# Retention followed by a multiplicative FFN: attention by units of a chunk of two batches, with products grouped by tiling mode

## The chip, the cores and the metric

The kernel runs on one core of a Trainium2 chip. The metric is the device time of the program in microseconds (us). A core has five engines that run side by side, each through its own instructions in order: TensorE (PE in the profile; its weight loads are PEld), VectorE (DVE), ScalarE (ACT), GpSimd (POOL) and SyncE (SP), which here only issues transfers. TensorE's results go to PSUM, eight banks of 2 KB on each of 128 partitions; everything else lies in SBUF.

## The reference, cut to what matters

```python
def _attn_ref(q, k, v):                      # (8, 8, 576, 64) each: batch, head, position, dim
    scores = (1 / sqrt(64)) * (q @ k.T)
    gamma = 1.0 - 2.0 ** (-5.0 - arange(8))  # one a head
    rel = i - j
    Dmat = where(rel >= 0, gamma ** rel, 0.0)
    return (scores * Dmat) @ v

def reference(...):
    x = attn_out.transpose(0, 2, 1, 3).reshape(4608, 512)
    a = x @ w1                               # 512 x 1024
    b = x @ w2                               # 512 x 1024
    h = (a * b) @ w3                         # 1024 x 1024
    return h @ w_out                         # 1024 x 512
```

The weights are float64; the kernel reads their 32-bit words and makes float32 of them on the chip. All products are in float32; each shows as two MATMUL records in the trace (two passes).

## The kernel before, in words

**Retention by chunks.** Each batch of 576 positions is cut into five chunks (`NC`), the first of 64 positions and four of 128. Because gamma^(i-j) = gamma^i * gamma^-j, the kernel scales q by gamma^i / 8 and v by gamma^-j and needs three things for a chunk: scores within the chunk, masked to j <= i, times v; q times the state, which is the sum of k v^T over the earlier chunks; and the state's own growth. The result is made transposed, (head, dim) on partitions, four pairs of heads (`NP`) of 128 rows each, as the FFN takes it.

The unit of attention is one chunk of one batch, 40 units `g`, and four functions make it:

- `front(g)` (line 105): GpSimd scales v (L110), TensorE transposes k and q in pairs of heads into `tp` tiles (L118), ScalarE copies k's out (L122), VectorE copies q's out and scales them on the way (L124, with `gq`, which eight broadcast loads, L86, fill at the start).
- `score(g)` (line 127): per pair of heads two products (L135), the first on the upper 64 rows of the array and the second on the lower 64, into two PSUM tiles `sc0` and `sc1`; VectorE multiplies by the mask into `pm` (L138).
- `state(g)` (line 142): eight products (L154) of 128 rows on the left or right 64 columns of the array grow the state in its own PSUM bank, which ScalarE copies to `sb` (L158) for the next chunk.
- `pv(g)` (line 161): for each head in turn a product of the state with q on a 64x64 quarter (L171, only two of the four quarters are ever used), and right behind it the product of v with the masked scores on a 128x64 half (L173), both added up in one PSUM tile `xps`, which ScalarE copies to `xT` (L176).

**Weights.** 40 blocks of 128 rows by 512 columns: 8 + 8 of w1 and w2, 8 of w_out, 16 of w3. `load_block` (L199) loads one on SP's queue into one of three `raw` tiles, `convert_block` (L209) makes float32 of it in seven VectorE instructions (L219 to L231) and starts the next load. w3 and w_out are multiplied out once: `w3_tr` (L241) transposes a row block of w3 on TensorE (L247), `w3_mm` (L253) makes the product (L256).

**FFN.** A pair of batches has 1152 tokens, three blocks (`NB`) of 384. `up(i, n, f)` (L266) makes 128 columns of x w1 and x w2 with four products each (L275); ScalarE copies the first (L279) and VectorE multiplies it with the second into `ab` (L280). `down(i, n, t)` (L282) makes 128 tokens of output with eight products (L286), ScalarE copies them out (L289), SP stores them (L291). A block has eight `up`s and three `down`s.

**The order is written out by hand** (`manual_schedule`): each engine does its instructions in the order in which the program emits them. The loop from line 315 goes over the units: it loads unit g+3, converts up to five blocks ahead, does `front(g+2)`, then a third of the FFN work due in this unit, `score(g+1)` and `state(g+1)`, a third, `pv(g)`, and the last third. After the last chunk of the first batch of a pair one FFN block comes due, after that of the second the other two; the w3 steps stand in the first pair's list, behind the first eight `up`s. PSUM is split into pools: two banks for transposes, two for scores, one for the state, three for everything else (lines 68 to 71).

Of the kernel before, what the change touches and what calls it, by code (L numbers as in the profile page):

```python
# [15 lines left out]
# Retention, by chunks of up to 128 positions. With gamma^(i-j) = gamma^i * gamma^-j,  # L16
#   out_i = sum_{j<=i in the chunk} (scale gamma^i q_i . k_j) (gamma^-j v_j)
#         + (scale gamma^i q_i) @ sum_{j in earlier chunks} k_j (gamma^-j v_j)^T,
# so the state of the earlier chunks only grows by sums, in PSUM. The output is
# made transposed, (h d) on partitions, as the first products of the FFN take x.  # L20
# FFN: ((x w1) * (x w2)) (w3 w_out), with w3 w_out multiplied out once.
# The weights come as the words of float64 and are rounded to the nearest float32 here.
@with_exitstack
def kernel(
# [19 lines left out]
    CV = 512                       # columns of weights converted at a time  # L44
    P = 128
    NP = H // 2                    # pairs of heads; pair p has rows p*128.. of x^T
    # chunks of a batch, the short one first: a short one after a state would have two
    # products of different rows of the array add up in one PSUM bank
# [4 lines left out]
    G = B * NC  # L53
    NB = 3                         # FFN blocks of a pair of batches
    TB = 2 * S // NB               # tokens of a block
# [6 lines left out]
    raw = ctx.enter_context(tc.tile_pool(name="raw", bufs=3))  # L62
    wst = ctx.enter_context(tc.tile_pool(name="wst", bufs=2))
    ld = ctx.enter_context(tc.tile_pool(name="ld", bufs=3))
# [3 lines left out]
    tp_ps = ctx.enter_context(tc.tile_pool(name="tp_ps", bufs=2, space=PSUM))  # L68
    sc_ps = ctx.enter_context(tc.tile_pool(name="sc_ps", bufs=1, space=PSUM))
    st_ps = ctx.enter_context(tc.tile_pool(name="st_ps", bufs=1, space=PSUM))  # L70
    ac_ps = ctx.enter_context(tc.tile_pool(name="ac_ps", bufs=3, space=PSUM))
# [9 lines left out]
    gk = const.tile([P, NC, H], F32, tag="gk", name="gk")  # L81
    for c in range(NC):
        nc.scalar.dma_start(gk[:sizes[c], c, :], decay_k[starts[c]:starts[c] + sizes[c], :])
    gq = const.tile([P, NP, S], F32, tag="gq", name="gq")
    for h in range(H):
        nc.scalar.dma_start(gq[heads[h % 2], h // 2, :],  # L86
                            decay_q[h:h + 1, :].to_broadcast([D, S]))
# [4 lines left out]
    wo = xp.tile([P, KD * 2 * S], F32, tag="xT", name="wo")[:, :KF * DM].rearrange(  # L92
        "p (g n) -> p g n", g=KF)
# [3 lines left out]
    def load(g):  # L97
        b, c = divmod(g, NC)
        sz = sizes[c]
        for nm, src, bufs in (("k", k, 3), ("q", q, 2), ("v", v, 2)):  # L100
            t = ld.tile([P, H, D], F32, tag="ld_" + nm, name="ld_" + nm, bufs=bufs)
            nc.sync.dma_start(t[:sz], src[b, :, starts[c]:starts[c] + sz, :].rearrange("h p d -> p h d"))
            live[nm, g] = t

    def front(g):
        c = g % NC
        sz = sizes[c]
        kn, qn, vn = live["k", g], live["q", g], live["v", g]
        vs = fr.tile([P, H, D], F32, tag="vs", name="vs", bufs=3)
        nc.gpsimd.tensor_tensor(out=vs[:sz], in0=vn[:sz],  # L110
                                in1=gk[:sz, c, :].unsqueeze(2).to_broadcast([sz, H, D]),
                                op=ALU.mult)
        kT = fr.tile([P, NP, P], F32, tag="kT", name="kT")
        qT = fr.tile([P, NP, P], F32, tag="qT", name="qT", bufs=3)
        for src, dst in ((kn, kT), (qn, qT)):
            tp = tp_ps.tile([P, NP, P], F32, tag="tp", name="tp")
            for p in range(NP):
                nc.tensor.transpose(tp[:, p, :sz],  # L118
                                    src[:sz, 2 * p:2 * p + 2, :].rearrange("p a d -> p (a d)"),
                                    ident[:sz, :sz])  # L120
            if dst is kT:
                nc.scalar.copy(kT[:, :, :sz], tp[:, :, :sz])  # L122
            else:
                nc.vector.tensor_mul(qT[:, :, :sz], tp[:, :, :sz], gq[:, :, starts[c]:starts[c] + sz])  # L124
        live["kT", g], live["qT", g], live["vs", g] = kT, qT, vs

    def score(g):
        c = g % NC
        sz = sizes[c]
        kT, qT = live["kT", g], live["qT", g]  # L130
        pm = fr.tile([P, 2, NP, P], F32, tag="pm", name="pm")
        sc = [sc_ps.tile([P, NP, P], F32, tag=f"sc{j}", name=f"sc{j}") for j in range(2)]
        for p in range(NP):
            for j, hs in enumerate(heads):
                nc.tensor.matmul(sc[j][:sz, p, :sz], kT[hs, p, :sz], qT[hs, p, :sz],  # L135
                                 start=True, stop=True)
        for j in range(2):
            nc.vector.tensor_mul(pm[:sz, j, :, :sz], sc[j][:sz, :, :sz],  # L138
                                 mask[:sz, :sz].unsqueeze(1).to_broadcast([sz, NP, sz]))
        live["pm", g] = pm  # L140

    def state(g):
        c = g % NC
        sz = sizes[c]
        if c == NC - 1:
            return
        kn, vs = live["k", g], live["vs", g]
        if c == 0:
            live["st"] = st_ps.tile([P, NP, D], F32, tag="st", name="st")
        st = live["st"]  # L150
        # one start a half: it clears the whole bank's flags on that half
        for p in range(NP):
            for j, hs in enumerate(heads):
                nc.tensor.matmul(st[hs, p, :], kn[:sz, 2 * p + j, :], vs[:sz, 2 * p + j, :],  # L154
                                 start=(c == 0 and p == 0), stop=(c == NC - 2),
                                 skip_group_check=True)
        sb = fr.tile([P, NP, D], F32, tag="sb", name="sb", bufs=3)
        nc.scalar.copy(sb, st)  # L158
        live["sb", g + 1] = sb

    def pv(g):
        b, c = divmod(g, NC)
        sz = sizes[c]
        qT, vs, pm = live["qT", g], live["vs", g], live["pm", g]
        if c == 0 and b % 2 == 0:
            live["xT", b // 2] = xp.tile([P, NP, 2 * S], F32, tag="xT", name="xT")
        xps = ac_ps.tile([P, NP, P], F32, tag="ac", name="xps")
        for p in range(NP):
            for j, hs in enumerate(heads):
                if c > 0:  # L170
                    nc.tensor.matmul(xps[hs, p, :sz], live["sb", g][hs, p, :], qT[hs, p, :sz],  # L171
                                     start=True, stop=False)
                nc.tensor.matmul(xps[hs, p, :sz], vs[:sz, 2 * p + j, :], pm[:sz, j, p, :sz],  # L173
# [209 lines left out]
```

## Time and profile before

| | |
|---|---|
| time, median of 3 runs | 1219.13 us (1218.30 to 1220.98) |
| the profiled execution's own time (its span) | 1218.3 us |
| TensorE busy | 1140.2 us, 94% |
| VectorE busy | 279.7 us, 23% |
| ScalarE busy | 132.0 us, 11% |
| GpSimd busy | 43.1 us, 4% |
| moved by the DMA queues | 60.67 MB |
| granted TensorE clock, mean | 0.951 |

In the profile a line such as `L275 PE MATMUL up<-xT,w_sb` names the line of the kernel, the engine, the operation and the tiles written and read. A timeline row begins with the start and the length in us; in square brackets stands the idle time before it and what ended it. Matmuls are pipelined and their ends are modelled, so the time that one takes in a stream is read from start to start. The row of 40 slices gives busy tenths, and PEclk the clock that TensorE was granted, in tenths of full speed.

### The profile page before, as it was taken

How to read it: one execution, taken by the hardware profiler on the slowest of the kernel's cores; microseconds unless marked ns; L12 is line 12 of the kernel's file. 1: busy time of each engine (PE TensorE's matmuls, PEld its weight loads, DVE VectorE, ACT ScalarE, POOL GpSimd, SP SyncE). 2: the span in 40 equal slices, each digit the busy share in tenths (PEclk: the TensorE clock that was granted, in tenths of full speed). 3: DMA queues.
4: the chain of work that ended last, by engine and by line, in shares of the span. 5: the costliest groups of instructions: out<-in, count | busy, mean ns of one | idle time of the engine just before them, and what ended most of it. 6: DMA issues, size and time to landing. Idle time of an engine off the chain costs nothing.

```text
span 1218.3 us, 11481 instructions
## 1 busy us (share of the span) xinstructions
PE 1140.2 (94%) x4928; PEld 630.8 (52%) x4928; DVE 279.7 (23%) x505; ACT 132.0 (11%) x261; POOL 43.1 (4%) x47
## 2 busy tenths in 40 slices
PE   3467897979999999999999999999999999999998
PEld 2234553434555555655655556555545556545454
DVE  2999716550110110110101101111101111101010
ACT  1000111101111111101101011111111111000000
POOL 1000000000000000000000000000000000000000
PEclk9555898989999999999999999999999999999999
DMA  8555601410202103103102002112021020000000
GB/s 199 147 154 156 153 14 52 113 43 18 61 1 65 26 9 69 32 16 71 27 9 65 18 18 61 40 43 61 1 59 33 1 63 15 1 27 1 26 0 26
DMA packets 124803, 60.67 MB, mean 50 GB/s; under 512 B 114512, under 2 KB 114512, under 8 KB 124752
## 3 DMA queue, kind: packets, MB, share of 16 engines
q1 hardware_dynamic: 123456, 58.73, 19.2%
q10 hardware_dynamic: 1296, 1.20, 0.4%
q8 instruction: 39, 0.64, 0.2%
q14 instruction: 12, 0.10, 0.0%
HBM read 50.48 MB, written 9.44 MB: 49 GB/s over the span
## 4 chain that ended last, share of the span: by engine, by line
PE 86%; DVE 12%; DMA 1%; issue 0%; ACTq 0%; ACT 0%; POOL 0%; DVEq 0%; POOLq 0%
PE up L275 40%; PE po L286 21%; PE xps L173 7%; PE xps L171 7%; PE ps L256 4%; PE sc L135 3%; PE tp L118 2%; DVE m L229 2%; DVE e L224 2%; DVE e L221 1%; DVE e L222 1%; PE st L154 1%; DVE m L227 1%; DVE e L219 1%; DVE w_sb L231 1%; DMA gq<-decay_q_dram 1%
## 5 line engine op out<-in xcount | busy, mean ns | idle before, releaser
L275 PE MATMUL up<-xT,w_sb 128*128 128x384 f32 x1536 | 514.1, 491 | 3.2 <-DVE ab L280 3.2
L275 PEld LDWEIGHTS up<-xT,w_sb 128*128 128x128 f32 x1536 | 288.0, 191 | 196.4 <-issue 5.9
L286 PE MATMUL po<-w3o,ab 128*128 128x512 f32 x576 | 254.0, 595 | 0.0
L280 DVE TENSOR_TENSOR ab<-up,a 128x384 f32<-128x384 f32 x96 | 53.4, 557 | 560.0 <-PE up L275 560.0
L286 PEld LDWEIGHTS po<-w3o,ab 128*128 128x128 f32 x576 | 107.6, 190 | 127.7 <-issue 124.8
L173 PE MATMUL xps<-pm,vs 128*64 128x128 f32 (+1 forms) x640 | 124.3, 298 | 0.0
L171 PE MATMUL xps<-qT,sb 64*64 64x128 f32 x512 | 118.0, 313 | 0.0
L124 DVE TENSOR_TENSOR qT<-tp,gq 128x512 f32<-128x512 f32 (+1 forms) x40 | 25.5, 637 | 253.9 <-PE tp L118 236.5
L173 PEld LDWEIGHTS xps<-pm,vs 128*64 128x64 f32 (+1 forms) x640 | 56.3, 141 | 52.9 <-issue 52.8
L171 PEld LDWEIGHTS xps<-qT,sb 64*64 64x64 f32 x512 | 51.3, 140 | 61.8 <-issue 61.5
L135 PE MATMUL sc<-qT,kT 64*128 64x128 f32 (+1 forms) x640 | 48.5, 290 | 33.3 <-DVE pm L138 33.2
L279 ACT COPY a<-up 128x384 f32<-128x384 f32 x96 | 46.0, 479 | 308.1 <-PE up L275 302.5
L110 POOL TENSOR_TENSOR vs<-ld_v,gk 128x512 f32<-128x512 f32 (+1 forms) x40 | 42.2, 1054 | 990.1 <-PE xps L173 629.4
L135 PEld LDWEIGHTS sc<-qT,kT 64*128 64x128 f32 (+1 forms) x640 | 40.4, 191 | 55.8 <-DVE pm L138 34.7
L138 DVE TENSOR_TENSOR pm<-sc,mask 128x512 f32<-128x512 f32 (+1 forms) x80 | 47.1, 630 | 74.1 <-PE sc L135 73.7
L256 PE MATMUL ps<-wo,w3T 128*128 128x512 f32 x128 | 59.7, 622 | 0.0
L289 ACT COPY ot<-po 128x512 f32<-128x512 f32 x36 | 21.1, 586 | 266.0 <-PE po L286 245.9
L176 ACT COPY xT<-xps 128x512 f32<-128x512 f32 (+1 forms) x40 | 21.8, 544 | 249.0 <-PE xps L173 249.0
L118 PE MATMUL tp<-ident,ld_k 128*128 128x128 f32 (+1 forms) x160 | 26.2, 291 | 17.6 <-DMA ld_k<-in_k_dram 17.6
L256 PEld LDWEIGHTS ps<-wo,w3T 128*128 128x128 f32 x128 | 25.2, 202 | 29.0 <-issue 29.0
L118 PEld LDWEIGHTS tp<-ident,ld_k 128*128 128x128 f32 (+1 forms) x160 | 19.4, 153 | 30.8 <-issue 29.2
L229 DVE SCALAR_TENSOR_TENSOR m<-raw,m 128x512 f32<-128x512 uint32 x40 | 28.5, 713 | 1.4
(28 smaller groups left out, 285.9 us busy)
## 6 DMA issues: line engine op xcount, KB each, us to landing
raw<-in_moe_w_dram SPq DMA_DIRECT2D x32, 512.0 KB, 3.6
out_dram<-ot SPq DMA_DIRECT2D x36, 256.0 KB, 2.1
ld_k<-in_k_dram SPq DMA_DIRECT2D x32, 256.0 KB, 3.6
ld_q<-in_q_dram SPq DMA_DIRECT2D x32, 256.0 KB, 4.4
ld_v<-in_v_dram SPq DMA_DIRECT2D x32, 256.0 KB, 4.6
raw<-in_moe_w_out_dram SPq DMA_DIRECT2D x8, 512.0 KB, 3.5
gq<-decay_q_dram ACTq DMA_DIRECT2D x8, 144.0 KB, 7.1
ld_k<-in_k_dram SPq DMA_DIRECT2D x8, 128.0 KB, 3.0
```

What stands on the lines that cost most here:

```text
L110: nc.gpsimd.tensor_tensor(out=vs[:sz], in0=vn[:sz], in1=gk[:sz, c, :].unsqueeze(2).to_broadcast([sz, H, D]), op=ALU.mult)
L118: nc.tensor.transpose(tp[:, p, :sz], src[:sz, 2 * p:2 * p + 2, :].rearrange("p a d -> p (a d)"), ident[:sz, :sz])
L135: nc.tensor.matmul(sc[j][:sz, p, :sz], kT[hs, p, :sz], qT[hs, p, :sz], start=True, stop=True)
L138: nc.vector.tensor_mul(pm[:sz, j, :, :sz], sc[j][:sz, :, :sz], mask[:sz, :sz].unsqueeze(1).to_broadcast([sz, NP, sz]))
L171: nc.tensor.matmul(xps[hs, p, :sz], live["sb", g][hs, p, :], qT[hs, p, :sz], start=True, stop=False)
L173: nc.tensor.matmul(xps[hs, p, :sz], vs[:sz, 2 * p + j, :], pm[:sz, j, p, :sz], start=(c == 0), stop=True)
L229: vec.scalar_tensor_tensor(m.bitcast(F32), in0=lo.bitcast(U32), scalar=2.0 ** -32, in1=m, op0=ALU.mult, op1=ALU.add)
L256: nc.tensor.matmul(ps, live["w3T", ft][:, g, :], wo[:, g, :], start=(g == 0), stop=(g == KF - 1))
L275: nc.tensor.matmul(t, w[:, c, f * P:(f + 1) * P], xT[:, c, n * TB:(n + 1) * TB], start=(c == 0), stop=(c == KD - 1))
L279: nc.scalar.copy(a, ps[0])
L280: nc.vector.tensor_mul(live["ab", i, n][:, f, :], ps[1], a)
L286: nc.tensor.matmul(po, ab[:, f, t * P:(t + 1) * P], w3o[:, f, :], start=(f == 0), stop=(f == KF - 1))
```

## The change

1. **Units.** A unit is now a chunk of two batches at once (`NB2` = 4 pairs, 20 units), so every load, tile and loop of `front`, `score`, `state` and `pv` covers 16 heads. k, q and v are loaded 512 KB at a time (128 positions); k has two tiles, q one, v three.
2. **Scaling of q.** GpSimd scales q and v in place, before the transposes. The factors `gq` now lie by position: one load of 18 KB, five small transposes and ten small copies make them. ScalarE copies both k's and q's transposes out.
3. **Grouping.** `pv` first does all products with the state, then all products with v. The products with the state run on all four 64x64 quarters: for two of the four pairs of heads (`r` = 1) a head's result goes to the other half of the partitions. Two PSUM banks take the results, one for each `r`. The halves so swapped are undone by loading the two halves of those rows of w1 and w2 swapped as well. `state` and `score` follow `pv` directly, in that order.
4. **PSUM.** One pool of seven banks takes everything but the state.
5. **Fewer weight tiles.** `raw` has two tiles for three, `exp` and `man` one for two, w3's row block `w3` and `w3T` one for two. `wo` has a tile of its own.
6. **Order.** The FFN of a pair becomes due only when both its batches are through. In the first pair's list come eight `up`s that need only the first half of w1 and w2, eight with the second half, then w3's steps, then the `down`s of two blocks, then the third block. While there is no FFN work (the first five units) two blocks are converted per unit, then six. The work of a unit is cut in two halves instead of three parts.

```diff
-    raw = ctx.enter_context(tc.tile_pool(name="raw", bufs=3))
-    wst = ctx.enter_context(tc.tile_pool(name="wst", bufs=2))
+    raw = ctx.enter_context(tc.tile_pool(name="raw", bufs=2))
+    wst = ctx.enter_context(tc.tile_pool(name="wst", bufs=1))
...
+    acc = ctx.enter_context(tc.tile_pool(name="acc", bufs=7, space=PSUM))
...
+        for nm in names:
+            t = ld.tile([P, 2 * H, D], F32, tag="ld_" + nm, name="ld_" + nm,
+                        bufs={"k": 2, "q": 1, "v": 3}[nm])
+            nc.sync.dma_start(
+                t[:sz], src[nm][2 * i:2 * i + 2, :, starts[c]:starts[c] + sz, :].rearrange("b h p d -> p (b h) d"))
...
+        for t, gam in ((qn, gq), (vn, gk)):
+            nc.gpsimd.tensor_tensor(
+                out=t[:sz], in0=t[:sz],
+                in1=gam[:sz, c].rearrange("p b h -> p (b h)").unsqueeze(2).to_broadcast([sz, 2 * H, D]),
+                op=ALU.mult)
...
     def pv(g):
...
-        for p in range(NP):
-            for j, hs in enumerate(heads):
-                if c > 0:
-                    nc.tensor.matmul(xps[hs, p, :sz], live["sb", g][hs, p, :], qT[hs, p, :sz],
-                                     start=True, stop=False)
-                nc.tensor.matmul(xps[hs, p, :sz], vs[:sz, 2 * p + j, :], pm[:sz, j, p, :sz],
-                                 start=(c == 0), stop=True)
...
+        banks = [acc.tile([P, 2, 2, P], F32, tag="acc", name="xps") for r in range(2)]
+        order = [(b, n) for b in range(2) for n in range(2)]
+        if c > 0:
+            for m, (b, n) in enumerate(order):
+                for r, j in ((0, 0), (0, 1), (1, 0), (1, 1)):
+                    p = 2 * r + n
+                    nc.tensor.matmul(banks[r][heads[j ^ r], b, n, :sz], live["sb", g][heads[j], b, p, :],
+                                     qT[heads[j], b, p, :sz], start=(m == 0), stop=False,
+                                     skip_group_check=True)
+        for m, (b, n) in enumerate(order):
+            for r in range(2):
+                for half in range(2):
+                    p, j = 2 * r + n, half ^ r
+                    nc.tensor.matmul(banks[r][heads[half], b, n, :sz], vs[:sz, b * H + 2 * p + j, :],
+                                     pm[:sz, b, j, p, :sz], start=(c == 0 and m == 0), stop=True,
+                                     skip_group_check=True)
...
+        for half in range(2):
+            for n in range(2):
+                for f in range(half * KF // 2, (half + 1) * KF // 2):
+                    add(up, i, n, f)
+        rest = [(up, i, 2, f) for f in range(KF)]
+        add(w3_tr, 0)
+        for ft in range(KF):
+            add(w3_mm, ft)
+            if ft + 1 < KF:
+                add(w3_tr, ft + 1)
+        for n in range(NB):
+            if n == 2:
+                for x in rest:
+                    add(*x)
+            for t in range(NT):
+                add(down, i, n, t)
...
     for g in range(G):
...
+            load(g + 2, "kv")
         if g + 1 < G:
+            front(g + 1)
+        if g + 2 < G:
+            load(g + 2, "q")
+
+        rows = min(turned[0] + 1, KF)
+        convert_up_to(min(2 * (g + 1) if g < NC else 2 * NC + 6 * (g - NC + 1),
+                          at["w3", rows - 1, DF - CV] + 1))
+        work((n + 1) // 2)
+        pv(g)
+        if g + 1 < G:
+            state(g + 1)
             score(g + 1)
+        work(n // 2)
         if c == NC - 1:
+            add_blocks(g // NC)
     work(len(todo))
```

More of the change, by code (lines that the diff above doesn't have):

```diff
@@ L303, in work @@
             todo.pop(0)()
[L305 to L309 removed]
+    load(0, "kqv")
+    load_block()
+    load(1, "kv")
+    load_block()
     front(0)
[L312 removed]
+    load(1, "q")
+    state(0)
     score(0)
[L314 removed]
     for g in range(G):
```

182 lines of the change are left out of this document (82 added, 100 removed).

## The prediction

> **What bounds the kernel now.** I read the page of the profile first, to see which engine is full and when.
>
> ```profile
> span 1218.3 us, 11481 instructions
> PE   3467897979999999999999999999999999999998
> DVE  2999716550110110110101101111101111101010
> PEclk9555898989999999999999999999999999999999
> ```
>
> From slice 10 (305 us) to the end TensorE is full at full clock. Before that VectorE is full in slices 1 to 3, TensorE runs at half clock there, and slices 5 to 8 (152 to 274 us) show holes on TensorE. So there are two stages: a head set by VectorE and loads, and a long stage where every us taken off TensorE comes off the span. The busy time by stretches (columns: stretch, length, then busy us of TensorE, weight loads, VectorE, ScalarE, GpSimd; granted clock, DMA share, GB/s) gives the period of a pair of batches and the holes:
>
> ```profile
> 0.00:30.00 30.00, 10.32 (x112) 8.29 (x112) 8.46 (x17) 4.53 (x8) 4.56 (x10) 1.00 0.89 200
> 66.00:87.50 21.50, 14.89 (x72) 8.79 (x72) 20.64 (x39) 1.33 (x3) 1.04 (x1) 0.50 0.49 141
> 186.00:210.00 24.00, 16.68 (x73) 8.74 (x72) 14.12 (x27) 2.13 (x4) 0.00 (x0) 0.79 0.14 45
> 230.00:260.00 30.00, 22.08 (x73) 11.21 (x71) 19.83 (x38) 2.25 (x4) 0.00 (x0) 0.83 0.33 87
> 574.70:834.60 259.90, 259.90 (x1185) 144.74 (x1185) 31.56 (x54) 30.32 (x62) 10.42 (x11) 1.00 0.16 37
> ```
>
> A pair of batches takes 259.9 us, all of it TensorE. The chain of waits gives the price of an `up`, a `down` and of w3's steps:
>
> ```profile
> 604.06 10.32 PE up L275 x32
> 621.45 6.87 PE po L286 x16
> 237.09 0.87 PE tp L247 x8
> 237.97 6.87 PE ps L256 x16
> 1194.08 20.61 PE po L286 x48
> ```
>
> The 32 are two `up`s, so 5.16 us each; a `down` is 6.87. A pair has 24 and 9: 24 x 5.16 + 9 x 6.87 = 185.7 us of FFN, which leaves 259.9 - 185.7 = 74.2 us for ten attention units, 7.4 each. The timeline of one unit shows where they go:
>
> ```profile
> 584.93 1.16 PE L135 MATMUL sc<-qT,kT 64*128 64x128 f32 x16
> 586.02 0.69 PE L154 MATMUL st<-vs,ld_k 128*64 128x64 f32 x16
> 586.63 10.59 PE L275 MATMUL up<-xT,w_sb 128*128 128x384 f32 x32
> 603.03 0.60 PE L118 MATMUL tp<-ident,ld_k 128*128 128x128 f32 x4
> 603.46 0.60 PE L118 MATMUL tp<-ident,ld_q 128*128 128x128 f32 x4
> 628.25 0.43 PE L171 MATMUL xps<-qT,sb 64*64 64x128 f32 x2
> 628.61 0.43 PE L173 MATMUL xps<-pm,vs 128*64 128x128 f32 x2
> 634.02 6.28 PE L286 MATMUL po<-w3o,ab 128*128 128x512 f32 x14
> ```
>
> Read start to start. Four transposes of 128 columns take 603.46 - 603.03 = 0.43 us, 0.109 each: the price of a pass of 128 columns alone. A float32 product is two passes. The 16 score passes take 586.02 - 584.93 = 1.09 us, under 16 x 0.109 = 1.74: L135 alternates between the two row halves of the array and two passes run side by side (8 x 0.109 = 0.87, and 0.22 to drain). The 16 state passes (64 columns, two column halves) take 0.61. But the output products take 634.02 - 628.25 = 5.77 us for 32 passes: L171 (a 64x64 tile) and L173 (128x64) alternate, each change of mode costs 628.61 - 628.25 = 0.36 us for two passes worth 0.22, and nothing runs side by side. That is 5.77 of a 128-row unit's 8.4.
>
> **The change part by part.** *Output products.* A unit is now a chunk of two batches. Its 32 state passes come first, on four quarters of the array, then its 32 passes with v on two column halves. Two batches cost 2 x 5.77 = 11.5 us before. Now: four at a time 8 x 0.109 = 0.87; two at a time 16 x 0.109 = 1.74. No row shows four at a time. The bounds are 0.87 and, with no overlap, 32 x 0.109 = 3.49; score's row, where two row halves overlap fully, is the nearest and I take 0.87. *State and score.* They follow directly: 16 x 0.0545 = 0.87 (64 columns) and 16 x 0.109 = 1.74, and the unit's transposes stay 16 x 0.109 = 1.74. *Changes of mode.* Into the run, between its kinds and out of it, five at about 0.18 (from 0.36 - 0.22 = 0.14 and score's 0.22): 0.9. Sum 0.87 + 1.74 + 0.87 + 1.74 + 1.74 + 0.9 = 7.9 us. A pair has a short unit (0.87 each for transposes, v, state and score at half the columns, no product with the state, 0.8 of changes: 4.3), three of 7.9 and a last one without a new state, 7.0: 35 us instead of 74.2.
>
> On the quarters a page speaks against the sum. Each output bank now receives from two row halves at once, on different partitions, which no product of this trace does: score's two row halves write separate tiles. The Trainium skill, TensorEngine Tiling (Array Packing), Gotcha 1: PSUM Pressure, says that different row tiles cannot access one PSUM bank simultaneously; by that rule the products of one bank would go one after the other. The Trainium skill, PSUM — Partial Sum Buffer, on bank collisions, counts by bank and 32-partition quadrant instead, by which nothing collides. No run here shows either.
>
> *q's scaling* leaves VectorE (L124) for GpSimd, and the copy for ScalarE, which is busy 30.3 of a pair's 259.9 us. In the long stage both hide. GpSimd's two multiplications are each twice as long as L110's.
>
> *Queues and slots.* On SP's queue k and v of the unit after next now stand ahead of its q, and q, with one tile, waits for the transposes of the q before it; weight loads and outputs queue behind. In the long stage that wait ends with the transposes at the head of a unit's iteration, and the loads have the rest of it, some 40 us of TensorE work ((185.7 + 35) / 5 = 44). Transposes, scores, outputs and FFN take turns in one pool of seven banks: a transpose can wait for a mask, which VectorE, 31.6 us busy of 259.9, ends in time there; not so while it converts.
>
> *The head.* The FFN now starts when both batches of the first pair are through, with ten weight blocks converted instead of 25. One iteration is two conversions and four masks on VectorE. Timeline and groups:
>
> ```profile
> 30.18 1.04 POOL L110 TENSOR_TENSOR vs<-ld_v,gk 128x512 f32<-128x512 f32 x1 [4.01 <-DMA ld_v<-in_v_dram]
> 30.27 1.50 DVE L229 SCALAR_TENSOR_TENSOR m<-raw,m 128x512 f32<-128x512 uint32 x1
> 34.86 0.69 DVE L229 SCALAR_TENSOR_TENSOR m<-raw,m 128x512 f32<-128x512 uint32 x1
> 45.54 0.41 DVE L219 TENSOR_SCALAR e<-raw 128x512 int32<-128x512 int32 x1
> 49.32 0.42 DVE L219 TENSOR_SCALAR e<-raw 128x512 int32<-128x512 int32 x1
> L138 DVE TENSOR_TENSOR pm<-sc,mask 128x512 f32<-128x512 f32 x64 | 41.2, 685 | 25.9 <-PE sc L135 25.9
> L138 DVE TENSOR_TENSOR pm<-sc,mask 64x256 f32<-64x256 f32 x16 | 6.0, 411 | 48.2 <-PE sc L135 47.7 <-POOL vs L110 0.4
> gq<-decay_q_dram ACTq DMA_DIRECT2D x8, 144.0 KB, 7.1
> ```
>
> The eight broadcast loads of gq on ScalarE's queue go; one of 18 KB, ten small ones of gk, five transposes and ten tiny copies come, before the first q has landed. A conversion is 49.32 - 45.54 = 3.78 us, a mask 0.685. And a GpSimd operation robs VectorE: the same L229 took 1.50 instead of 0.69 beside one of 1.04 us. Two of twice the length cost 4 x 0.81 = 3.2 an iteration. So 7.6 + 2.7 + 3.2 = 13.5 us, against loads of 1.57 MB of q, k, v and 1.05 MB of weights, 2.6 MB at the first row's 200 / 0.89 = 225 GB/s: 11.6 us. VectorE sets the pace, narrowly. The Trainium skill, SBUF — State Buffer, Who interferes with whom, says that GpSimd and VectorE share a port pair as an exclusive lock held for a whole instruction; by it the theft could reach the full 4.2 an iteration and the head be 4 us longer.
>
> The first q of 128 rows lands behind 3.4 MB (15 us, and some 3 to start) and is scaled (2.1); turning, copying and the scores, partly at half clock, are put at 7, so the scores of unit 1 stand at about 28 and its masks end at 31. Three iterations more: 71. Unit 5's four short masks (0.41 each) wait for two conversions and the theft, and free the PSUM slots that the first `up` needs: 71 + 7.6 + 1.6 + 3 = 83. With no theft it would be 72; with the clock at half throughout (below) 92.
>
> ```profile
> 45.08 2.67 PE L135 MATMUL sc<-qT,kT 64*128 64x128 f32 x16 [16.16 <-DVE pm L138]
> 124.14 11.57 PE L275 MATMUL up<-xT,w_sb 128*128 128x384 f32 x32
> 143.38 4.52 PE L275 MATMUL up<-xT,w_sb 128*128 128x384 f32 x8 [3.19 <-DVE ab L280]
> 200.21 1.08 PE L247 MATMUL tp<-ident,w 128*128 128x128 f32 x4 [4.62 <-DVE w L231]
> raw<-in_moe_w_dram SPq DMA_DIRECT2D x32, 512.0 KB, 3.6
> ```
>
> Half clock shows as 2.67 for scores that take 1.16. TensorE's 7.9 us of an iteration would be about 15.
>
> *Conversions after the head.* 30 blocks are left where 15 were, with two raw tiles for three and one w3 and one w3T tile for two. A block's load lands in 3.6 us, just under the conversion beside it. What cover is there: seven PSUM slots let TensorE run four `up`s (20.6 us) ahead of VectorE. Units 5 and 6 each queue six conversions on VectorE (22.7, with the theft 26) ahead of the products that free PSUM: a stall of 5 and one of 4. The first w3 step issues four conversions only when it is reached, and TensorE waits them out: 4 x 3.78 = 15 and a copy, 16. The other seven rows have two conversions and a copy (8.3) against one product of 6.87: 1.5 each, more where masks or q's load on SP's queue come first (the next raw load stands there behind q's, which waits for that tile's last transposes): 14. Idle 39. The clock falls after each longer hole: clock 0.79 over 24 us and 0.83 over 30 are about 10 us at half, 5 lost, behind holes of about 5. Four such holes here: 16. Stalls 55 in all.
>
> *Sum.* 83 to the first `up`; FFN 4 x 185.7 + w3's 8 x (6.87 + 0.87) = 804.6; three pairs of attention, 105, less 5 that is done before 83; stalls 55; behind the last product 1218.3 - (1194.08 + 20.61) = 3.6. Together 1046 us on the profile's own time; the median of the runs shown, 1219.13, is 0.8 above the profiled 1218.3, so 1047. The same sum for the kernel before: 124.1 + 804.6 + 35 units x 7.42 (five are through by then) - 3 + 3.6 = 1189, so 29 of stalls and half clock, which the holes of slices 5 to 8 bear out.
>
> **The rivals.** *The quarters run two at a time* (the bank rule, as a mechanism of this kernel): 16 x 0.109 instead of 8, 0.87 for 12 units, +10: 1057. For it: no row has two row halves on one bank. Chance 0.15.
>
> *The grouping ends the mode changes but not the waiting of one pass for the next*: 3.49 for 0.87 and 3.49 for 1.74, +4.4 for 12 units: 1099. Against it: score and state passes overlap today. 0.06.
>
> *Head and conversions cost less*: GpSimd robs nothing (72), conversions hide but for the first w3 row: stalls 35, 1016. 0.07.
>
> *Slower: conversions in series with TensorE.* If with two raw tiles each of the 30 conversions waits for its own load and TensorE for it, 30 x (3.78 + 3.6) = 221 us in place of 39: 1047 + 182 = 1229. It decides as soon as a raw load, behind q, k, v on SP's queue, lands later than the next conversion ends, and that in nearly every block. Against it: 3.6 is under 3.78, and four `up`s of lead. 0.04.
>
> **How the numbers follow.** My forecast, 1047, has chance 0.68, with 1020 to 1075 by head (72 to 92) and stalls (40 to 70). The range 1012 to 1098 takes in the second and the cheaper head. All cases but one lie far under 1219: faster by over 0.2% (about what a measurement of this kernel can tell from no change) 0.95, within it 0.01, slower 0.04.
>
> **What would show it.** Right: a pair's period of 185.7 + 35 = 221 us; state passes of a unit in about 1.0 us and those with v in about 1.8 where both took 11.5; the first `up` at 83; a hole of some 16 us ahead of the first w3 transposes, and half clock behind it. Wrong: state passes of a unit at 1.8 or more (the quarters), a period over 225, a first `up` after 92, holes ahead of most w3 rows longer than 4 us, or a granted clock under 1 in the full stage.

## The result, and the profile after

The changed kernel takes 1033.55 us (median of 4 runs, 1031.75 to 1036.30) against 1218.83 for the kernel before: a ratio of 0.848, with an interval of 0.846 to 0.849. The forecast was 1047, in a range of 1012 to 1098. The profiled execution took 1034.25 us, of which the trace spans 1032.4.

The same lines of the page as before:

```profile
span 1032.4 us, 11355 instructions
PE   4869998498899999999999999999999999999998
DVE  4898456767800010101110100101101001000010
PEclk8888999698999999999999999999999999999999
```

(A slice is now 25.8 us.) The head is three slices long where it was five, the holes behind it stand in slices 3 to 10, and from slice 11 (284 us) TensorE is full. The chain of waits shows the kinds of products of a 128-row unit of two batches:

```profile
474.82 1.03 PE xps L189 x32
475.85 1.90 PE xps L196 x32
477.75 0.93 PE st L169 x32
478.68 1.99 PE sc L148 x32
496.34 1.75 PE tp L133 x16
```

L189 holds the products with the state, L196 those with v. Together 2.93 us, where two units of the kernel before took 11.5. All five make 7.60 us of TensorE for two batches. Stretches of the profile (length, then busy us of TensorE, weight loads, VectorE, ScalarE, GpSimd; clock, DMA share, GB/s):

```profile
81.75:290.44 208.69, 176.88 (x850) 103.25 (x850) 139.33 (x246) 26.93 (x53) 16.02 (x9) 0.93 0.33 96
406.84:627.49 220.65, 220.65 (x1186) 131.53 (x1185) 24.74 (x44) 33.25 (x68) 18.79 (x10) 1.00 0.18 44
```

The second row is one period of a pair of batches, 220.65 us instead of 259.9, all TensorE at full clock. The first row goes from the first `up` to the first `down`: 208.69 - 176.88 = 31.8 us in which TensorE stood still. Its timeline has the places (in brackets the idle time before the row, and who ended it):

```profile
81.75 24.69 PE L300 MATMUL up<-xT,w_sb 128*128 128x384 f32 x72
108.88 2.85 PE L300 MATMUL up<-xT,w_sb 128*128 128x384 f32 x8 [2.43 <-DVE ab L305]
169.76 4.50 PE L300 MATMUL up<-xT,w_sb 128*128 128x384 f32 x8 [2.92 <-DVE ab L305]
197.85 1.08 PE L278 MATMUL tp<-ident,w 128*128 128x128 f32 x4 [12.38 <-DVE w L262]
201.75 1.08 PE L278 MATMUL tp<-ident,w 128*128 128x128 f32 x4 [2.81 <-DVE w L262]
233.92 0.63 PE L278 MATMUL tp<-ident,w 128*128 128x128 f32 x4 [3.41 <-DVE w L262]
237.82 1.08 PE L278 MATMUL tp<-ident,w 128*128 128x128 f32 x4 [3.28 <-DVE w L262]
```

The first `up` starts at 81.75 us. The two runs of six conversions cost 2.43 and 2.92 us, the four conversions ahead of the first w3 step 12.38 + 2.81 = 15.2, and w3's other rows the rest, 11.2.

### The profile page after: what moved, and what is told of

It is laid out like the page before. It is cut to its first block, busy times and chain, and to the rows that moved or that the text cites. A ratio compares the mean times of both kernels' runs of the same rounds, so it can differ in the third digit from the quotient of the medians.

```text
span 1032.4 us, 11355 instructions
## 1 busy us (share of the span) xinstructions
PE 966.2 (94%) x4933; PEld 570.8 (55%) x4933; DVE 269.3 (26%) x475; ACT 144.1 (14%) x285; POOL 78.4 (8%) x47
## 4 chain that ended last, share of the span: by engine, by line
PE 82%; DVE 12%; DMA 3%; issue 1%; SPq 1%; ACT 0%; ACTq 0%; POOL 0%; DVEq 0%; POOLq 0%
PE up L300 44%; PE po L311 24%; PE ps L287 4%; PE xps L196 3%; PE sc L148 3%; DVE e L255 2%; PE tp L133 2%; DMA raw<-in_moe_w_dram 2%; DVE m L260 2%; DVE e L250 2%; PE st L169 1%; DVE m L258 1%; PE xps L189 1%; DVE e L252 1%; DVE e L253 1%; DVE pm L151 1%
## 5 line engine op out<-in xcount | busy, mean ns | idle before, releaser
L300 PE MATMUL up<-xT,w_sb 128*128 128x384 f32 x1536 | 504.6, 489 | 5.4 <-DVE ab L305 5.4
L122 POOL TENSOR_TENSOR ld_q<-ld_q,gq 128x1024 f32<-128x1024 f32 (+1 forms) x20 | 38.7, 1935 | 645.3 <-DMA ld_q<-in_q_dram 638.6
L133 PE MATMUL tp<-ident,ld_q 128*128 128x128 f32 (+1 forms) x160 | 22.1, 287 | 20.1 <-POOL ld_q L122 20.1
L122 POOL TENSOR_TENSOR ld_v<-ld_v,gk 128x1024 f32<-128x1024 f32 (+1 forms) x20 | 39.5, 1975 | 2.3 <-DMA ld_v<-in_v_dram 2.3
L148 PE MATMUL sc<-qT,kT 64*128 64x128 f32 (+1 forms) x640 | 39.1, 273 | 0.0
L196 PE MATMUL xps<-pm,ld_v 128*64 128x128 f32 (+1 forms) x640 | 37.8, 273 | 0.0
L196 PEld LDWEIGHTS xps<-pm,ld_v 128*64 128x64 f32 (+1 forms) x640 | 33.4, 143 | 5.0 <-issue 5.0
L278 PE MATMUL tp<-ident,w 128*128 128x128 f32 x64 | 10.7, 303 | 25.2 <-DVE w L262 25.1
L255 DVE SCALAR_TENSOR_TENSOR e<-raw,e 128x512 int32<-128x512 int32 x40 | 32.6, 814 | 1.4
L133 PEld LDWEIGHTS tp<-ident,ld_q 128*128 128x128 f32 (+1 forms) x160 | 18.6, 153 | 21.4 <-POOL ld_q L122 21.4
```

The source lines that it names most:

```text
L122: nc.gpsimd.tensor_tensor(out=t[:sz], in0=t[:sz], in1=gam[:sz, c].rearrange("p b h -> p (b h)").unsqueeze(2).to_broadcast([sz, 2 * H, D]), ...
L133: nc.tensor.transpose(tp[:, p, :sz], src[:sz, h:h + 2, :].rearrange("p a d -> p (a d)"), ident[:sz, :sz])
L148: nc.tensor.matmul(sc[j][:sz, p, :sz], kT[hs, b, p, :sz], qT[hs, b, p, :sz], start=True, stop=True)
L196: nc.tensor.matmul(banks[r][heads[half], b, n, :sz], vs[:sz, b * H + 2 * p + j, :], pm[:sz, b, j, p, :sz], start=(c == 0 and m == 0), stop ...
L255: vec.scalar_tensor_tensor(e, in0=hi, scalar=-(1 << 31), in1=e, op0=ALU.bitwise_and, op1=ALU.bitwise_or)
L300: nc.tensor.matmul(t, w[:, c, f * P:(f + 1) * P], xT[:, c, n * TB:(n + 1) * TB], start=(c == 0), stop=(c == KD - 1))
```

## The experiments

**First: grouping alone, in the kernel before.** Units, pools and order as before; only `pv` does all products with the state first.

```diff
-        for p in range(NP):
-            for j, hs in enumerate(heads):
-                if c > 0:
+        if c > 0:
+            for p in range(NP):
+                for j, hs in enumerate(heads):
                     nc.tensor.matmul(xps[hs, p, :sz], live["sb", g][hs, p, :], qT[hs, p, :sz],
-                                     start=True, stop=False)
+                                     start=(p == 0), stop=False, skip_group_check=True)
+        for p in range(NP):
+            for j, hs in enumerate(heads):
                 nc.tensor.matmul(xps[hs, p, :sz], vs[:sz, 2 * p + j, :], pm[:sz, j, p, :sz],
-                                 start=(c == 0), stop=True)
+                                 start=(c == 0 and p == 0), stop=True, skip_group_check=True)
```

> The kernel before with one edit: in each unit of one batch all products with the state come first and then all products with v, on the same two quarters and two halves as before; nothing else of the change. Theory (the 0.36 us of every two passes is the change of tiling mode, and it also keeps neighbours from running side by side): a 128-row unit's output products go from 5.77 us to about 0.87 + 0.87 + 0.3 = 2.1; some 28 of the 32 such units lie in the stage where TensorE is full, so 28 x 3.7 = 103 us less, 1116 us. Rival (0.36 us is what two dependent passes into one PSUM tile take, whatever stands beside them, and the gain came from the larger units and the shorter head): within 10 us of 1219.

Measured 1117.11 us, ratio 0.917 (0.915 to 0.918). The timeline of a unit:

```profile
585.51 1.09 PE L171 MATMUL xps<-qT,sb 64*64 64x128 f32 x16
586.53 1.09 PE L175 MATMUL xps<-pm,vs 128*64 128x128 f32 x16
587.55 7.13 PE L288 MATMUL po<-w3o,ab 128*128 128x512 f32 x16
```

From start to start 587.55 - 585.51 = 2.04 us for the 32 passes that took 5.77. The same products with the same operands cost about a third once their modes are sorted; the rival, by which the 0.36 us belonged to the products themselves, falls. Nor is it the wait of v's product for the state's product that it is added to: in the kernel before, the next head's product with the state, which goes to other partitions, also starts 0.36 us behind (628.97 - 628.61; the prediction shows the two rows ahead of it):

```profile
628.97 0.43 PE L171 MATMUL xps<-qT,sb 64*64 64x128 f32 x2
```

This one edit is worth 102 of the 185 us. It also answers the question of the banks: the state's 16 passes here run on two row halves that write one tile of one bank, on different partitions, and take 586.53 - 585.51 = 1.02 us, under 16 x 0.109 = 1.74.

**Second: two quarters at a time, in the changed kernel.**

```diff
-            for m, (b, n) in enumerate(order):
-                for r, j in ((0, 0), (0, 1), (1, 0), (1, 1)):
-                    p = 2 * r + n
+            for r in range(2):
+                for m, (b, n) in enumerate(order):
+                    for j in range(2):
+                        p = 2 * r + n
...
```

> The changed kernel with the products with the state in another order: first all of one output bank, which use the quarters (0,0) and (1,1), then all of the other, which use (0,1) and (1,0), so that no more than two quarters can work at once. Theory (four at a time today): L189's run of 32 passes goes from 1.03 us to about 16 x 0.109 + 0.15 = 1.9, 0.87 us for 12 units in the full stage, 10 us more and up to 3 in the head: 1044 to 1047 us. Rival (two row halves on one bank already take turns, and 1.03 us has another reason): no change, 1033 us.

Measured 1040.22 us, ratio 0.854 (0.852 to 0.857), clear of the changed kernel's 0.846 to 0.849. Its timeline:

```profile
475.64 1.59 PE L190 MATMUL xps<-qT,sb 64*64 64x128 f32 x32
477.16 1.97 PE L197 MATMUL xps<-pm,ld_v 128*64 128x128 f32 x32
```

The state's run takes 477.16 - 475.64 = 1.52 us where it took 1.03: 0.49 for 12 units, 6 us, and 7 were measured. So the quarters do work four at a time in the changed kernel, and two products of different row halves write one PSUM bank (on different partitions) side by side. The single records of the two traces bear this out: in the changed kernel four passes start within 0.02 us, every 0.109 us. The size was off: 1.52 is less than the 1.9 expected for two at a time. In this run's records two passes start every 0.109 us at first, but four do from 476.13 to 476.52, then two again: the products of the second bank begin before those of the first are through.

**Third: alternating again, in the changed kernel.**

```diff
+                    if c > 0:
+                        nc.tensor.matmul(banks[r][heads[half], b, n, :sz], live["sb", g][heads[j], b, p, :],
+                                         qT[heads[j], b, p, :sz], start=(m == 0), stop=False,
+                                         skip_group_check=True)
                     nc.tensor.matmul(banks[r][heads[half], b, n, :sz], vs[:sz, b * H + 2 * p + j, :],
```

(The loop over the state's products ahead of it is gone.)

> The changed kernel with each product with the state followed at once by the product with v of the same head, so that the tiling mode changes at every product as in the kernel before; units, pool and order otherwise as changed. Theory: 32 groups of two passes at 0.36 us, 11.5 us for a 128-row unit instead of 2.9: 8.6 for 12 units in the full stage, 103 us more, and up to 25 in the head: 1137 to 1162 us. Rival (larger units matter, grouping little): under 1060 us.

Measured 1152.95 us, ratio 0.946 (0.944 to 0.947): 119 us more than the changed kernel. Each two passes take 0.36 us again:

```profile
74.76 0.43 PE L190 MATMUL xps<-qT,sb 64*64 64x128 f32 x2
75.11 0.43 PE L193 MATMUL xps<-pm,ld_v 128*64 128x128 f32 x2
75.48 0.43 PE L190 MATMUL xps<-qT,sb 64*64 64x128 f32 x2
```

From both sides, then, the order of the products carries most of the gain; all the rest of the change, without it, brings 66 us.

**Fourth: conversions spread.** Behind each of the first twelve `up`s come one or two conversions; the next w3 row is converted right behind this row's transposes; the last four `up`s stand between w3's rows.

```diff
+        for x, (n, f) in enumerate(ups[:12]):
+            add(up_then_convert, i, n, f, 10 + (16 * (x + 1) + 11) // 12)
...
+        for ft in range(KF):
+            add(tr_then_convert, ft)
+            add(w3_mm, ft)
+            if ft % 2 == 0:
+                add(up, i, *ups[12 + ft // 2])
...
-        convert_up_to(min(2 * (g + 1) if g < NC else 2 * NC + 6 * (g - NC + 1),
-                          at["w3", rows - 1, DF - CV] + 1))
+        convert_up_to(min(2 * (g + 1), 2 * NC))
```

> The changed kernel with the conversions after the head spread: one or two behind each of the first twelve ups instead of six at the start of a unit and four in front of the first w3 step; the two blocks of the next w3 row are converted right behind the transposes of this one; the four ups left over stand between w3's rows. Theory (the holes after the first up, 32 us, and the half clock behind them, some 10, come from when conversions are issued, VectorE having time enough): about 35 of these go, 1000 us, and the granted clock stays 1 from the first up. Rival (two raw tiles and the load behind them set the rate of conversion, whenever it is issued): the holes only move, 1020 us or more.

Measured 1015.14 us, ratio 0.833 (0.831 to 0.836): half of what was expected. From the first `up` to the first `down` TensorE stands still for 15.1 us where it was 31.8. The first two holes are gone; ahead of w3 there still are

```profile
160.43 1.08 PE L278 MATMUL tp<-ident,w 128*128 128x128 f32 x4 [4.43 <-DVE w L262]
164.67 1.08 PE L278 MATMUL tp<-ident,w 128*128 128x128 f32 x4 [3.16 <-DVE w L262]
```

The stretch from the first `up` to these transposes (columns as in the stretches above) shows why:

```profile
85.67:155.00 69.33, 69.33 (x303) 42.58 (x303) 58.67 (x111) 9.62 (x20) 3.81 (x3) 0.97 0.37 117
```

TensorE has no hole in it any more, though its clock is 0.97 and not 1, and VectorE is busy 58.67 of 69.33 us. All but 3 us of its idle time lies at the start, where the conversions stand behind the first `up`:

```profile
93.25 0.56 DVE L305 TENSOR_TENSOR ab<-up,a 128x384 f32<-128x384 f32 x1 [10.90 <-PE up L300]
```

From there on it was nearly full, and w3 came before it was through. The last experiment takes this up.

**Fifth: two tiles for q.** q is loaded together with k and v, ahead of the transposes of the q before it.

```diff
-                        bufs={"k": 2, "q": 1, "v": 3}[nm])
+                        bufs={"k": 2, "q": 2, "v": 3}[nm])
...
-    load(1, "kv")
+    load(1, "kqv")
...
-            load(g + 2, "kv")
+            load(g + 2, "kqv")
...
```

> The changed kernel with two tiles for q in place of one, and q loaded together with k and v, so that its load no longer waits for the transposes of the q before it. Theory (VectorE sets the pace of the head, as predicted): the first up stays at 80 to 84 us and the time within 3 us of 1033.6. Rival (q's chain of load, scaling, transposes and next load sets it; TensorE waited 2.8, 1.7, 2.2 and 5.0 us for GpSimd's q in the head): the first up comes at about 72 to 75 us, 1025 us.

Measured 1031.88 us, ratio 0.846 (0.845 to 0.848), not told apart from the changed kernel. The time is the theory's; the first `up`, at 77.96, is neither the theory's nor the rival's. In the changed kernel TensorE waited last for q, ahead of the first `up`, and GpSimd's scaling of that q for its load; the rows of TensorE, GpSimd and VectorE, then those of this run:

```profile
79.99 1.97 PE L133 MATMUL tp<-ident,ld_q 128*128 128x128 f32 x8 [4.99 <-POOL ld_q L122]
78.04 1.90 POOL L122 TENSOR_TENSOR ld_q<-ld_q,gq 128x1024 f32<-128x1024 f32 x1 [12.96 <-DMA ld_q<-in_q_dram]
76.81 1.40 DVE L151 TENSOR_TENSOR pm<-sc,mask 64x256 f32<-64x256 f32 x4
```

```profile
77.96 2.75 PE L300 MATMUL up<-xT,w_sb 128*128 128x384 f32 x8
80.94 1.40 DVE L151 TENSOR_TENSOR pm<-sc,mask 64x256 f32<-64x256 f32 x4
81.41 20.91 PE L300 MATMUL up<-xT,w_sb 128*128 128x384 f32 x64 [0.70 <-DVE pm L151]
109.48 5.09 PE L300 MATMUL up<-xT,w_sb 128*128 128x384 f32 x8 [7.16 <-DVE ab L305]
```

With q in time the first half of the first `up` starts at 77.96, and its second half waits for masks. These end later than in the changed kernel, at 82.3 instead of 78.2: GpSimd now scales at other moments, and up to these masks VectorE's conversions lost 16.8 us to it, where they lost 8.1 in the changed kernel (each row's time over what the same operation takes alone, added up; the sixth experiment has the rows). The hole behind the six conversions grew from 2.43 to 7.16 us. A wait was taken away and others grew in its place.

The head also differs from run to run. In the fourth and the eleventh experiment its code is that of the changed kernel, and the first `up` came at 85.67 and 81.44, with 12.8 and 9.3 us lost in this way. So a few us in the head show nothing by themselves.

**Sixth: without scaling.**

```diff
-        for t, gam in ((qn, gq), (vn, gk)):
+        for t, gam in ():
```

> The changed kernel without GpSimd's two multiplications of a unit: q and v go unscaled into the products, which leaves the decays out of the output. Theory (GpSimd robs VectorE of about 3.2 us a unit in the head, and 3 to 4 in each of the two runs of six conversions behind it): the first up comes at about 70 us and the holes behind it shrink by some 5, 1017 us. Rival (the loads set the pace of the head, 11.6 us a unit of 128 positions): the first up not before 78 us, 1028 us or more.

Measured 1019.45 us, ratio 0.836 (0.835 to 0.837): 14 us less. What GpSimd does to VectorE is plain in the changed kernel's timeline; first GpSimd's rows, then VectorE's:

```profile
40.91 1.90 POOL L122 TENSOR_TENSOR ld_q<-ld_q,gq 128x1024 f32<-128x1024 f32 x1 [7.62 <-DMA ld_q<-in_q_dram]
51.62 2.44 POOL L122 TENSOR_TENSOR ld_q<-ld_q,gq 128x1024 f32<-128x1024 f32 x1 [6.95 <-DMA ld_q<-in_q_dram]
60.85 1.92 POOL L122 TENSOR_TENSOR ld_q<-ld_q,gq 64x1024 f32<-64x1024 f32 x1 [4.94 <-DMA ld_q<-in_q_dram]
62.74 2.34 POOL L122 TENSOR_TENSOR ld_v<-ld_v,gk 64x1024 f32<-64x1024 f32 x1
```

```profile
40.84 2.48 DVE L151 TENSOR_TENSOR pm<-sc,mask 128x512 f32<-128x512 f32 x4
44.12 0.83 DVE L250 TENSOR_SCALAR e<-raw 128x512 int32<-128x512 int32 x1 [0.80 <-DMA raw<-in_moe_w_dram]
52.21 2.48 DVE L151 TENSOR_TENSOR pm<-sc,mask 128x512 f32<-128x512 f32 x4
61.06 2.27 DVE L255 SCALAR_TENSOR_TENSOR e<-raw,e 128x512 int32<-128x512 int32 x1
63.25 2.12 DVE L258 TENSOR_SCALAR m<-raw 128x512 int32<-128x512 int32 x1
66.74 2.48 DVE L151 TENSOR_TENSOR pm<-sc,mask 128x512 f32<-128x512 f32 x4
```

L255 and L258 take 0.69 and 0.42 us alone (their rows at 57.16 and 57.76); here 3.3 us are lost beside two multiplications of 4.26. The masks, which read PSUM, take the same 2.48 beside GpSimd (at 40.84 and 52.21) as without (at 66.74). So the loss hangs on what VectorE does at that moment: the multiplications at 40.91 and 42.77 fell beside masks, and only L250 lost 0.4 us (0.83 for 0.43). Without scaling, the first `up` comes at 73.54 instead of 81.75 and waits for a load:

```profile
71.81 1.94 PE L133 MATMUL tp<-ident,ld_q 128*128 128x128 f32 x8 [4.07 <-DMA ld_q<-in_q_dram]
73.54 25.16 PE L300 MATMUL up<-xT,w_sb 128*128 128x384 f32 x72
```

So VectorE and GpSimd set the head's pace, with the loads close behind: 8 us of the 14 came in the head, not the 12 expected of it, and the two holes behind six conversions, 2.43 and 2.92, shrank to 0.16 and nothing. The run also takes GpSimd's 1.9 us out of q's own way to the transposes, which it does not tell apart from what VectorE gains.

**Seventh: PSUM split as before.** Two banks for transposes, two for scores, three for the rest.

```diff
-    acc = ctx.enter_context(tc.tile_pool(name="acc", bufs=7, space=PSUM))
+    tp_ps = ctx.enter_context(tc.tile_pool(name="tp_ps", bufs=2, space=PSUM))
+    sc_ps = ctx.enter_context(tc.tile_pool(name="sc_ps", bufs=2, space=PSUM))
+    acc = ctx.enter_context(tc.tile_pool(name="acc", bufs=3, space=PSUM))
...
```

> The changed kernel with PSUM split as before: two banks for transposes, two for scores, three for everything else, instead of one pool of seven. Theory (the one pool is what lets a unit's four transposes, four score tiles and two outputs follow each other without waiting, and gives the four ups of lead during conversions): about 1 us for transposes waiting on copies and 1 to 2 us for scores waiting on masks, 2.5 a unit for 15 units, and ten more behind conversions: 1070 to 1085 us. Rival (waits on PSUM hide behind the loads of weights and copies end in time): within 8 us of 1033.6.

Measured 1093.62 us, ratio 0.897 (0.896 to 0.898), 60 us more, and 9 over the range that was expected. Its timeline behind the runs of conversions and in the full stage:

```profile
116.69 15.23 PE L302 MATMUL up<-xT,w_sb 128*128 128x384 f32 x40 [12.44 <-DVE ab L307]
191.46 15.40 PE L302 MATMUL up<-xT,w_sb 128*128 128x384 f32 x40 [12.58 <-DVE ab L307]
700.06 1.16 PE L150 MATMUL sc<-qT,kT 64*128 64x128 f32 x16
702.00 1.75 PE L150 MATMUL sc<-qT,kT 64*128 64x128 f32 x16 [0.78 <-DVE pm L153]
703.68 15.75 PE L302 MATMUL up<-xT,w_sb 128*128 128x384 f32 x48
```

Scores take 703.68 - 700.06 = 3.62 us instead of 1.99, since the second batch's tiles wait for the first's masks, and the two holes that were 2.43 and 2.92 are over 12: three slots instead of seven leave TensorE fewer `up`s of lead. With units of two batches the one pool is no detail.

**Eighth: three raw tiles.** `bufs=3` for 2 in the changed kernel's `raw` pool.

> The changed kernel with three raw tiles in place of two; nothing else. Theory (a raw load that waits for its tile holds the next unit's k, v and q behind it on SP's queue, up to 7 us at the end of the head, and the next raw load stands behind q's): the first up comes 3 to 6 us earlier and the holes of 3 us at w3's rows shrink, the hole of 12 ahead of the first w3 step stays: about 1025 us. Rival (two tiles suffice, since a load lands in 3.6 us beside a conversion of 3.78): within 3 us of 1033.6.

Measured 1034.82 us, ratio 0.849 (0.847 to 0.850): no difference, as the rival had it. VectorE no longer waited for raw loads in the head, where two such waits of the changed kernel took 0.80 and 1.69 us. But its conversions lost 14.5 us to GpSimd up to unit 5's masks instead of 8.1, and the first `up` came at 84.06 us, behind a wait of 4.24 us for these masks, not earlier.

**Ninth: the fourth and the fifth together.**

> The changed kernel with the spread conversions of the fourth experiment and the two q tiles of the fifth. If the two act on different places (holes behind the first up; the end of the head), their gains add: 1015.1 - 1.7 = 1013 us. If the shorter head only moves a hole, as the fifth experiment's wait on q became one on masks: 1015 us.

Measured 1015.12 us, ratio 0.832 (0.830 to 0.834): no further gain over the fourth. The two expectations, 1013 and 1015, both lie in its interval, so the time does not decide between them. In the trace the two waits ahead of w3 are 5.49 and 6.31 us where they were 4.43 and 3.16.

**Tenth: q scaled by ScalarE**, on top of the ninth (which its expectation calls the eleventh).

```diff
-        for t, gam in ((qn, gq), (vn, gk)):
+        for t, gam in ((vn, gk),):
...
+            if dst is qT:
+                for b in range(2):
+                    for h in range(H):
+                        nc.scalar.mul(qn[:sz, b * H + h, :], qn[:sz, b * H + h, :], gq[:sz, c, b, h:h + 1])
...
```

> As the eleventh, but q is scaled by ScalarE in sixteen small instructions a unit, behind the copies of k's transposes, and GpSimd scales v alone. Theory (GpSimd robs VectorE; without any scaling the changed kernel lost 14 us): half the theft goes, 5 to 7 us less than the eleventh, 1006 us. Rival (sixteen instructions of ScalarE, ahead of q's transposes in every unit of the head, take longer than GpSimd's one of 1.9 us and TensorE waits for them): no gain or a loss, 1013 us or more.

Measured 1087.78 us, ratio 0.892 (0.890 to 0.894): 73 us more than the ninth, far worse than the rival said. The group of ScalarE's multiplications, then the sixteen of one unit and q's transposes behind them in the full stage:

```profile
L132 ACT ACTIVATE ld_q<-ld_q,gq 128x64 f32<-128x64 f32 x256 | 62.9, 341 | 0.0
814.86 3.93 ACT L132 ACTIVATE ld_q<-ld_q,gq 128x64 f32<-128x64 f32 x16
815.52 3.80 PE L137 MATMUL tp<-ident,ld_q 128*128 128x128 f32 x8 [1.26 <-ACT ld_q L132]
```

Sixteen multiplications, which overlap a little and take 3.93 us together, stand between k's copies and q's transposes on ScalarE, which does its instructions in order. So TensorE waits in the full stage too: q's eight transposes take 1.26 + 3.80 us instead of 0.87. In the changed kernel GpSimd scaled q as soon as it landed (its wait at 78.04 ended with the load), and in the period from 406.84 to 627.49 TensorE never waited for it. The theft was real, the cure was not.

**Eleventh: spread, with all sixteen `up`s ahead of w3.** The same sixteen conversions as in the fourth, over fourteen `up`s; no `up`s between w3's rows.

```diff
-        for x, (n, f) in enumerate(ups[:12]):
-            add(up_then_convert, i, n, f, 10 + (16 * (x + 1) + 11) // 12)
+        for x, (n, f) in enumerate(ups):
+            add(up_then_convert, i, n, f, min(26, 10 + (16 * (x + 1) + 13) // 14))
...
```

> As the fourth experiment, with all sixteen ups ahead of w3's first step and the same sixteen conversions spread over fourteen of them; no ups between w3's rows. In the fourth TensorE still waited 4.4 and 3.2 us ahead of the first w3 step, since VectorE needs some 76 us for those sixteen conversions, its masks and ab, and twelve ups with two attention units give about 75. Theory (VectorE is short of time there only because w3 comes too early): 20 us more of ups cover it, the wait ahead of the first w3 step goes, w3's rows wait 1 to 2 us each as in the changed kernel (some 12 in all), the sum about 1010 us. Rival (what is gained ahead of w3 is lost between its rows, where two conversions and a copy, 8.3 us, stand against 7.7 of TensorE): 1015 us or more.

Measured 1003.40 us, ratio 0.822 (0.820 to 0.824): the fastest of all, 30 us under the changed kernel. The timeline at the start of w3, and the longest wait of its rows:

```profile
178.10 1.04 PE L278 MATMUL tp<-ident,w 128*128 128x128 f32 x8
217.77 0.63 PE L278 MATMUL tp<-ident,w 128*128 128x128 f32 x4 [3.27 <-DVE w L262]
```

No wait is left ahead of the first step, and from the first `up` to the first `down` TensorE stands still for 6.9 us, where it was 31.8 in the changed kernel and 15.1 in the fourth experiment. So the holes came from when conversions were issued, and from w3 coming before VectorE could be through; the two raw tiles stayed as they were.

## Why the prediction was right, and where it was off

- **Attention.** Forecast 7.9 us for a unit and 221 for a period; measured 7.60 and 220.65. The value taken for the quarters, 0.87 plus a change of mode, showed as 1.03, that for v's passes, 1.74, as 1.90. The rule by bank, which the prediction weighs from the Trainium skill, TensorEngine Tiling (Array Packing), Gotcha 1: PSUM Pressure, does not hold for this case: two row halves share a bank, on different partitions, in the 1.03 us and in the 1.02 us of the first experiment. The trace agrees with the count by bank and 32-partition quadrant that the prediction takes from the Trainium skill, PSUM — Partial Sum Buffer, on bank collisions.
- **The head.** Forecast 83 us to the first `up`, measured 81.75, but in part by luck. The sum has 3.2 us lost to GpSimd in an iteration and lets the first `up` wait for unit 5's masks, which it has end at 83. They ended at 76.81 + 1.40 = 78.2. Behind unit 1's masks, forecast to end at 31 and measured at 32.9, the sum has 3 x 3.2 + 3 = 12.6 us lost; the rows show 5.0. The size put down, 3.2, came about only where both multiplications fell beside conversions (3.2 and 3.3); where they fell beside masks it was 0.3 to 1.0. What filled the gap is a wait that the sum does not have: the next unit's q, whose load landed at 78.0 and whose scaling ended at 79.9. That these two errors nearly cancel was not foreseen. The 4.2 that the prediction works out from the Trainium skill, SBUF — State Buffer, Who interferes with whom, was not reached in any iteration.
- **Stalls.** This is the term that was mis-sized: 55 us forecast. TensorE's idle time between the first `up` and the first `down` is 31.8 where 39 were put down (2.43 and 2.92 for 5 and 4, 15.2 for 16, 11.2 for 14). The sum leaves 1032.4 - 81.75 - 804.6 - 100 - 3.6 = 42.4 for stalls and half clock, so 10.6 are left for half clock, not 16. The clock was granted at half for 29.9 us of this stretch, in four pieces, and TensorE was busy for 16.2 of them, so some 8 us were lost to it; where the other 2.5 went stays open. The 12.6 us by which the term was too large are nearly all of the 13.6 between the sum's 1046 and the span of 1032.4. (The 0.8 that the prediction adds for the time over the span is 1034.25 - 1032.4 = 1.85 in the profiled execution.)
- **The rivals.** Two at a time fell with the 1.03 us. The passes without overlap fell with it and with v's 1.90. Conversions in series with TensorE did not come about: the two runs of conversions left holes under 3 us, with two raw tiles as with three. The cheaper head and conversions were the rival nearest to the truth, for the conversions' part: 42.4 us lie nearer to its 35 than to 55. Its other part, that GpSimd robs nothing, is wrong.

The sum was right because its largest term, TensorE's passes, came from rows of the same shapes, and the two uncertain terms, of which one was too large and the other met by luck, were small beside it.

## What to carry to other kernels

Where small products of different tile shapes alternate on TensorE, sort them by shape before anything else: here each alternation added 0.14 us to 0.22 of work and took away the side-by-side run of neighbouring tiles. When units are made larger, look at what queues behind them: PSUM slots, and work that is issued in a lump on the engine that frees them. At a stall ahead of a step that waits for prepared data, ask when that preparation was issued, and whether the step could simply come later. And a forecast that comes out is checked term by term: here the head's number held although the wait that ended it was another.

## What the runs showed of the hardware that was not expected

- With the order by bank, which names two quarters at a time, 32 passes took 1.52 us, under sixteen times the 0.109 us of a pass (1.74): in the middle of the run passes of both banks started side by side.
- Where GpSimd's multiplications ran beside conversions, which read SBUF alone, VectorE lost 3.3 us to 4.26 us of them; masks, which read PSUM, kept their 2.48 us for four. So the same two multiplications cost VectorE from 0.3 to 3.3 us by the moment at which they ran.
- A ScalarE multiplication of 128x64 with a factor for each partition took 0.341 us, and sixteen in a row 3.93 us, twice GpSimd's single one of 1.9 us.
